# Attention and an MLP in one kernel: plain products for the first output group, and another order of sums, copies and pieces

## The chip, the cores and the metric

The kernel runs on one core of a Trainium2 chip. The core has five engines that work side by side, each through its own queue: TensorE (PE in the profile, with its weight loads listed apart as PEld), VectorE (DVE), ScalarE (ACT), GpSimd (POOL) and SyncE (SP). POOL and SP mainly start DMA transfers here. The metric is the device time of one execution in microseconds (us). Before the change it was 392.39 us, the median of three runs (391.98 to 393.38).

## What is computed

Attention with a squared ReLU in place of a softmax, for 8 batches of 12 heads, 448 positions and a head size of 64; then a two-layer MLP with an exact GELU over the 8 x 448 = 3584 tokens.

```python
def _attn_ref(q, k, v):                  # 8 x 12 x 448 x 64 each
    S = q.shape[2]
    scale = 1.0 / np.sqrt(q.shape[-1])
    scores = scale * np.matmul(q, k.transpose(0, 1, 3, 2))
    attn = np.maximum(scores, 0.0) ** 2 / S
    return np.matmul(attn, v)

def _moe_ref(x, w_in, w_out):            # x: 3584 x 768, w_in: 768 x 2048, w_out: 2048 x 768
    h = x @ w_in
    g = 0.5 * h * (1.0 + erf(h / sqrt(2)))
    return g @ w_out
```

The attention's output, 12 heads of 64 side by side, is the x of the MLP. Inputs and output are float32.

## The kernel before

The matmuls are in bf16. The program is built by a small list scheduler: every piece of work is an `Op` with its possible engines and durations, the pieces that it depends on and the buffers that it needs and frees. The scheduler picks, for each engine, the piece that can start earliest by its own estimates (a `bias` shifts a piece's rank), and then writes the instructions in that order. At run time each engine works through its queue in that order. The order of PE and of POOL is fixed by hand (`pe_q`, `pool_q`); the scheduler decides the rest.

The parts that the change touches are these.

**The second layer by seven products.** The tokens are taken in 14 groups of 256 rows (two tiles of 128). For a group, the second layer is a product of 2 x 2 blocks: two row tiles, the 2048 inner columns in two halves, the 768 output columns in two halves. It is done by a scheme with seven block products in place of eight (a form of Strassen's scheme). That needs sums of weight blocks, made once, and sums of activation blocks for each group, both on DVE.

```python
    K2 = KF // 2                         # 8 slices of 128 inner columns
    quad = {(i, j): wout_sb[:, i*K2 : i*K2+K2, j*ND : j*ND+ND] for i in range(2) for j in range(2)}
    tsum = {n: wpool.tile([128, K2, ND], BF16, ...) for n in (1, 2, 4)}
    tsum[3] = quad[0, 1]                 # the third sum overwrites a block of the weights

    def add_tsums():                     # weight sums, in two parts each (x = 0, 1)
        def sub(n, c, a, b, deps):
            return sch.add((("DVE", 0.95, 1.07),),
                lambda e: V.tensor_sub(tsum[n][:, c], a[:, c], b[:, c]), deps, bias=SUM_BIAS)
        for x, c in enumerate((slice(0, 4), slice(4, K2))):
            ld = list(ld_wout.values())
            t1 = sub(1, c, quad[0, 1], quad[0, 0], ld[: x + 1])
            t2 = sub(2, c, quad[1, 1], tsum[1], [t1] + ld)
            t3 = sub(3, c, quad[1, 1], quad[0, 1], [t1] + ld)
            t4 = sub(4, c, quad[1, 0], tsum[2], [t2] + ld)
            SUMS[x] = [t1, t2, t3, t4]

    def add_group(g):
        # ... (cut) rows, buffers
        done = [o for (bb, *_), o in GL.items() if bb in bs] + SUMS[0] + SUMS[1]
        # ... (cut) activation sums, each a DVE tensor_tensor, with bias=SUM_BIAS
        s1 = sum_op(1, add, lambda: h(0, o2), lambda: h(1, o2), done)
        s2 = sum_op(2, sub, lambda: box["s", 1], lambda: h(0, o1), done + [s1])
        s3 = sum_op(3, sub, lambda: h(0, o1), lambda: h(0, o2), done)
        s4 = sum_op(4, sub, lambda: h(1, o1), lambda: box["s", 2], done + [s2])
        # ... (cut) product(): 8 matmuls into a PSUM bank; passed(): bank to SBUF, copied or added
        p1 = product("a", lambda: h(0, o1), quad[0, 0], done, need=("f",))
        v1 = passed("a", first, None, [p1], need=("p",))
        p6 = product("b", lambda: box["s", 2], tsum[2], done + [s2], need=("f",), frees=("s2",))
        v2 = passed("b", part(0, right), first, [v1, p6], need=("osb",))
        # ... (cut) p2, p7, p5, p4, p3 with their passes and the stores
        return [(1.3, o) for o in (p1, p6, p2, p7, p5, p4, p3)]
```

The PSUM banks of these products and of the first layer come from a pool of two (`f_pp`, "f").

**The copies and transposes of Q and K.** From batch 2 on, Q and K of a batch are loaded by POOL's queue (`nq`, `nk`), rearranged by DVE (`pk`, three copies; `pq`, six), and turned by seven DMA transposes on SP's queue (`kT`, `qT`). A tiny POOL copy (`gate`) holds the next batch's loads until the transposes are done.

**The order on PE.** Attention pieces (scores `ps` at L550, output `pav` at L612) and MLP pieces (first layer `psh` at L659, second layer `pso` at L752) are interleaved. While a batch's attention runs, the MLP pieces of the batch before are put between its steps, in proportion to their cost.

```python
    order = slots(2, B)                  # six slots for each batch from 2 on
    per = 2 * G
    GROUPS = {2: (0, 1), 3: (2, 3), 4: (4, 5), 5: (6,), 6: (7, 8), 7: (9, 10), 8: (11, 12, 13)}
    for b in range(2, B):
        add_steps(steps(b), dve=1)
        # ... (cut) copies, transposes and loads of later batches; at b == 2: add_tsums()
        x2 = [y for g in GROUPS[b] for y in add_group(g)]
        carry = x2[len(x2) - 7 + CARRY :]          # the last three products go to the next stage
        stage.append(atoms + x2[: len(x2) - 7 + CARRY])
    for n, slot in enumerate(order):
        # ... (cut) attention pieces of the slot
        while atoms and done < total * (n % per + 1) / per - 0.01:
            done += atoms[0][0]
            pe_q.append(atoms.pop(0)[1])
```

Of the kernel before, what the change touches and what calls it, by code (L numbers as in the profile page):

```python
# [13 lines left out]
KC = 112  # L14
NC = S // KC
# [33 lines left out]
DVE_STEPS = (1,)  # L49
HALF_M = 6  # L50
PASS_BIAS = -0.4
SUM_BIAS = 0.3
CARRY = 4


# [155 lines left out]
def kernel(  # L211
# [194 lines left out]
    def add_pk(b, g0, g1, after=(), bias=0.0):  # L406
        for g in range(g0, g1):
            deps = ld_k[b, g] + list(after)
            deps += [Tk[max(b - 1, 1), x, i][0] for x in range(G) for i in range(NK)]
            Pk[b, g] = sch.add(  # L410
                (("DVE", 0.31, 0.43),),
                lambda e, g=g: permute_k(V.tensor_copy, g, nk[b][:, 2 * g : 2 * g + 2]), deps,
                bias=bias,
            )

    def add_pq(b, g0, g1, c0=0, c1=NC, after=(), bias=0.0):
        for g in range(g0, g1):
            deps = [ld_q[b, g, c] for c in range(c0, c1)] + list(after)
            deps += [Tq[max(b - 1, 1), g, c][0] for c in range(c0, c1)]
            if b == 2:  # L420
                deps += [Tq[1, x, c][0] for x in range(G) for c in range(NC)]
            d = 2 * (0.07 + (c1 - c0) * 128 / 3840)

            def fn(e, g=g):
                permute_q(
                    V.tensor_copy, g, c0, c1, nq[b][:, 4 * g : 4 * g + 4, c0 * D : c1 * D]
                )

            op = sch.add((("DVE", d, d + 0.12),), fn, deps, bias=bias)
            for c in range(c0, c1):  # L430
                Pq[b, g, c] = op
# [59 lines left out]
    def add_T_dma(b, after):  # L491

        after = [list(x) for x in after]
        for g in range(G):
            def fn(e, g=g):
                nc.sync.dma_start_transpose(
                    get_T(b)[1][:, g].rearrange("p (i t) -> p i t", t=128), get_p()[1][:, g]
                )

            op = sch.add((("SP", 1.2, 3.0),), fn, [Pk[b, g]] + old_T(b) + after.pop(0))  # L500
            for i in range(NK):
                Tk[b, g, i] = (op, op)
        for c in range(NC):
            def fn(e, c=c):
                nc.sync.dma_start_transpose(get_T(b)[0][:, :, bass.ts(c, KC)], get_p()[0][:, c, :])  # L505

            op = sch.add((("SP", 1.2, 3.0),), fn, [Pq[b, g, c] for g in range(G)] + old_T(b) + after.pop(0))
            for g in range(G):
                Tq[b, g, c] = (op, op)
# [20 lines left out]
    def h_ring():  # L530

        if not hT:
            hT[0] = hpool.tile([128, KF, RING], BF16, tag="h", name="h_sb")
        return hT[0]
# [164 lines left out]
    def add_tsums():  # L699

        def sub(n, c, a, b, deps):
            return sch.add(
                (("DVE", 0.95, 1.07),),
                lambda e: V.tensor_sub(tsum[n][:, c], a[:, c], b[:, c]), deps, bias=SUM_BIAS,  # L704
            )

        for x, c in enumerate((slice(0, 4), slice(4, K2))):
            ld = list(ld_wout.values())
            t1 = sub(1, c, quad[0, 1], quad[0, 0], ld[: x + 1])
            t2 = sub(2, c, quad[1, 1], tsum[1], [t1] + ld)  # L710
            t3 = sub(3, c, quad[1, 1], quad[0, 1], [t1] + ld)
            t4 = sub(4, c, quad[1, 0], tsum[2], [t2] + ld)
            SUMS[x] = [t1, t2, t3, t4]

    osbs = {}

    def add_group(g):

# [4 lines left out]
        def h(i, o):  # L723
            return h_ring()[:, i * K2 : i * K2 + K2, o : o + 128]

        done = [o for (bb, *_), o in GL.items() if bb in bs] + SUMS[0] + SUMS[1]
        mine = []
        box = {}

# [17 lines left out]
        def product(bank, left, right, deps, need=(), frees=(), joint=()):  # L747
            def fn(e):
                if need:
                    box[bank] = f_pp.tile([128, NB], F32, tag="f", name="pso")  # L750
                for kf in range(K2):
                    nc.tensor.matmul(  # L752
                        box[bank][:, :ND],
                        left()[:, kf],
                        right[:, kf],
                        start=bool(need) and kf == 0,
                        stop=kf == K2 - 1,
                        skip_group_check=not need,
                    )

            d = K2 * (ND / 2400 + 0.0025)
            o = sch.add(
                (("PE", d, d + 0.24),), fn, deps, need=need, frees=frees, joint=joint, mode="F"
            )
            mine.append(o)
            return o

        def osb(x):
            if (g, x) not in osbs:
                osbs[g, x] = opool.tile([128, DM], F32, tag="osb", name="osb")  # L770
            return osbs[g, x]
# [20 lines left out]
            )  # L792

        def store(x, c, queues):
            def fn(e):
                queue, j = list(queues), rows[x][0]
                while j < rows[x][0] + 128:
                    bb, r = divmod(j, S)
                    k, p0 = divmod(r, KC)
                    m = min(KC - p0, rows[x][0] + 128 - j)  # L800
                    to = out[bb * S : (bb + 1) * S, :].rearrange("(p c) d -> c p d", c=NC)
                    y = j - rows[x][0]
                    queue.pop(0).dma_start(to[k, p0 : p0 + m, c], osb(x)[y : y + m, c])
                    j += m

            return fn

        left, right, full = slice(0, ND), slice(ND, DM), slice(0, DM)
        p1 = product("a", lambda: h(0, o1), quad[0, 0], done, need=("f",))
        v1 = passed("a", first, None, [p1], need=("p",))  # L810
        p6 = product("b", lambda: box["s", 2], tsum[2], done + [s2], need=("f",), frees=("s2",))
        p6.joint, s4.joint, s4.frees = [s4], [p6], ("s2",)
        v2 = passed("b", part(0, right), first, [v1, p6], need=("osb",))
        p2 = product("a", lambda: h(1, o1), quad[1, 0], [v1])
# [17 lines left out]
            readers.setdefault(bb, []).extend(mine)  # L832
        return [(1.3, o) for o in (p1, p6, p2, p7, p5, p4, p3)]

    def f1(b):
        return [(1.14, add_f1(b, m)) for m in range(KF)]

    def steps(b):
        return [((b, g, i, None),) for g in range(G) for i in range(NK)]
# [5 lines left out]
            tuple(x[n : n + 2]) for n in range(7, len(x), 2)  # L845
        ]

    def slots(first, last):


        out, done = [], None
        for b in range(first, last):
            for g in range(G):
                x = [("QK", (b, g, i, None)) for i in range(NK)]
                mid = ("AV", done) if done else ("FFN", None)
                out.append(x[:2] + [mid] + x[2:4])
                out.append(x[4:])
                done = (b, g, None)
        return out + [[("AV", done)]]


    nc.scalar.dma_start(k32, kv_view(k, 0, 0, 1))
# [85 lines left out]
        add_f1(0, m, bias=F1B_BIAS)  # L948


    order = slots(2, B)
    first = [next((x for kind, x in sl if kind == "QK"), None) for sl in order]
    per = 2 * G

    class at_slot:


        def __init__(self, n):
            self.key = first[n]

        @property
        def done(self):
            return QK[self.key].done

    def at(n):
        return [at_slot(min(n, len(first) - 2))]

    stage = []
    GROUPS = {2: (0, 1), 3: (2, 3), 4: (4, 5), 5: (6,), 6: (7, 8), 7: (9, 10), 8: (11, 12, 13)}
    add_load(3)  # L970
    for b in range(2, B):
        add_steps(steps(b), dve=1)
        if b + 1 < B:

            n = per * (b - 2) + {2: 2, 3: 2}.get(b, 1)
            add_pk(b + 1, 0, G, after=at(n))
            add_pq(b + 1, 0, G, after=at(n))
            add_T_dma(b + 1, [at(n + (y >= 4)) for y in range(7)])
            if b + 2 < B:
                add_gate(b + 1)  # L980
                add_load(b + 2)
        if b == 2:
            add_tsums()
            x1 = f1(b - 1)
            first_atoms, atoms = x1[:LEAD], x1[LEAD:]
        else:
            atoms = carry + f1(b - 1)
        x2 = [y for g in GROUPS[b] for y in add_group(g)]
        carry = x2[len(x2) - 7 + CARRY :]
        stage.append(atoms + x2[: len(x2) - 7 + CARRY])  # L990
    pe_q.extend(x[1] for x in first_atoms)
    for n, slot in enumerate(order):
        for kind, x in slot:
            if kind == "FFN":
                pe_q.append(stage[0].pop(0)[1])
            else:
                pe_q.append(AV[x] if kind == "AV" else QK[x])
        if n < per * len(stage):
            atoms = stage[n // per]
            if n % per == 0:  # L1000
                total, done = sum(x[0] for x in atoms), 0.0
            while atoms and done < total * (n % per + 1) / per - 0.01:
                done += atoms[0][0]
                pe_q.append(atoms.pop(0)[1])
    for _, o in carry + f1(B - 1) + [y for g in GROUPS[B] for y in add_group(g)]:
        pe_q.append(o)
    sch.run({"PE": pe_q, "POOL": pool_q})
# [28 lines left out]
```

## Time and profile before

| | before |
|---|---|
| time, median of 3 | 392.39 us |
| span of the profiled execution | 392.5 us |
| mean granted TensorE clock | 0.973 of full |
| PE busy, matmuls | 367.4 us, 3325 |
| DVE busy, instructions | 253.6 us, 456 |
| ACT busy, instructions | 200.6 us, 304 |
| weight sums, L704 | 8, about 0.95 us each |
| activation sums, L733 | 56, about 0.68 us each |

A line such as "93.83 2.74 PE L752 MATMUL ... x8 [13.02 <-DVE s_sb L733]" is a piece of the timeline: start, length, engine, line of the kernel, operation, output from inputs, how many instructions are merged, and in brackets the idle time of the engine before it and what ended that. "Line waited for" views give the total of such idle times, how many, and the longest. Busy time is instruction time; a PE that is busy at half clock is still busy, so the row of granted clock is read beside it. Idle time on an engine that does not set the end costs nothing.

### The profile page before, as it was taken

Reading aid. Unit: us, or ns where it says so; the run is one execution under the profiler, and the core shown is the slowest. Engines: PE = TensorE matmul, PEld = TensorE weight load, DVE = VectorE, ACT = ScalarE, POOL = GpSimd, SP = SyncE. Lnnn points to the kernel's source line nnn. Section 1 sums busy time; section 2 is a strip of 40 time slices with the busy share of each in tenths; the row PEclk is TensorE's granted clock in tenths of the full one; section 3 lists DMA queues with packets and bytes.
Section 4 is the critical chain, followed back from the end, with each engine's and each line's share of the span. In section 5 each row is a group of like instructions: output and inputs, shape, how many; then the busy total and the mean of one; then the engine's idle time right before and its main releaser. Section 6 shows DMA issues by size and latency. Waiting matters only on the chain.

```text
span 392.5 us, 7901 instructions
## 1 busy us (share of the span) xinstructions
PE 367.4 (94%) x3325; PEld 202.6 (52%) x3325; DVE 253.6 (65%) x456; ACT 200.6 (51%) x304; POOL 45.8 (12%) x69
## 2 busy tenths in 40 slices
PE   8799999924969999999999999999999999999995
PEld 7576544412535555555555445555555555555663
DVE  3899963476769457894488846963787438800662
ACT  4898855820524773456543776477345754144000
POOL 8665303100200002001100020000000000000000
PEclk9899999975989999999999999999999999999999
DMA  9999998999972168854950879280022001120232
GB/s 176 195 197 204 198 159 110 209 202 164 130 162 78 29 115 125 172 128 95 166 115 17 183 109 138 73 133 18 3 82 80 2 3 55 42 64 2 72 88 82
DMA packets 69523, 42.93 MB, mean 109 GB/s; under 512 B 37744, under 2 KB 66032, under 8 KB 69488
## 3 DMA queue, kind: packets, MB, share of 16 engines
q0 software_dynamic: 30512, 22.47, 38.4%
q1 hardware_dynamic: 38656, 19.46, 23.0%
q8 instruction: 26, 0.43, 0.4%
q10 hardware_dynamic: 320, 0.51, 0.4%
q14 instruction: 9, 0.07, 0.1%
HBM read 45.61 MB, written 11.01 MB: 144 GB/s over the span
## 4 chain that ended last, share of the span: by engine, by line
PE 81%; DMA 8%; DVE 5%; POOL 2%; ACT 1%; SPq 1%; issue 1%; POOLq 0%
PE pso L752 33%; PE psh L659 33%; PE ps L550 8%; DMA nq<-in_q_dram 7%; PE pav L612 7%; DVE a_sq L571 1%; SPq L505 1%; DVE s_sb L733 1%; DMA qT<-pq 1%; ACT a_sq L562 1%; POOL nk L348 1%; POOL v_sb L366 1%; DVE a_sq L564 1%; DVE t_sb L704 0%; DVE xT L314 0%
## 5 line engine op out<-in xcount | busy, mean ns | idle before, releaser
L562 ACT ACTIVATE a_sq<-ps 128x896 bf16<-128x896 f32 (+1 forms) x141 | 123.0, 914 | 72.8 <-PE ps L550 72.8
L659 PE MATMUL psh<-xT,win_sb 128*128 128x448 bf16 (+1 forms) x804 | 151.2, 345 | 0.1
L571 DVE TENSOR_TENSOR a_sq<-a_sq 128x896 bf16<-128x896 bf16 (+1 forms) x169 | 101.9, 617 | 43.1 <-ACT a_sq L562 42.0
L659 PEld LDWEIGHTS <-win_sb 128*128 128x128 bf16 x804 | 76.3, 98 | 71.2 <-issue 9.1
L669 ACT ACTIVATE h_sb<-psh 128x448 bf16<-128x448 f32 x128 | 70.1, 547 | 63.1 <-PE psh L659 52.9
L752 PEld LDWEIGHTS <-s_sb 128*128 128x128 bf16 x448 | 43.5, 99 | 48.2 <-DVE s_sb L733 16.8
L752 PE MATMUL pso<-t_sb,s_sb 128*128 128x384 bf16 x224 | 43.3, 339 | 16.0 <-DVE s_sb L733 16.0
L550 PE MATMUL ps<-qT,kT 64*64 64x448 bf16 (+1 forms) x756 | 48.0, 344 | 1.4 <-ACT qT L316 0.5
L752 PEld LDWEIGHTS <-h_sb 128*128 128x128 bf16 x336 | 32.4, 99 | 25.1 <-issue 4.6
L564 DVE TENSOR_SCALAR a_sq<-ps 128x896 bf16<-128x896 f32 x28 | 30.4, 1090 | 18.9 <-PE ps L550 18.4
L752 PE MATMUL pso<-wout_sb,h_sb 128*128 128x384 bf16 x224 | 41.9, 331 | 0.0
L752 PE MATMUL pso<-wout_sb,s_sb 128*128 128x384 bf16 x224 | 41.0, 326 | 0.0
L612 PE MATMUL pav<-a_sq,v_sb 64*64 64x448 bf16 (+1 forms) x756 | 37.3, 334 | 0.7 <-ACT a_sq L562 0.4
L786 DVE TENSOR_TENSOR osb<-pso,p_sb 128x384 f32<-128x384 f32 x42 | 23.4, 558 | 17.3 <-PE pso L752 15.6
L550 PEld LDWEIGHTS <-kT 64*64 64x64 bf16 x756 | 18.9, 108 | 23.0 <-issue 18.1
L612 PEld LDWEIGHTS <-v_sb 64*64 64x64 bf16 x756 | 21.7, 109 | 12.8 <-issue 2.0
L316 ACT CAST xT<-pav 128x448 bf16<-128x448 f32 (+1 forms) x25 | 12.4, 495 | 21.1 <-DVE xT L314 11.8
L314 DVE COPY p_sb<-pso 128x384 f32<-128x384 f32 x14 | 7.8, 557 | 22.8 <-PE pso L752 22.6
L517 POOL COPY gate<-qT 128x4 bf16<-128x4 bf16 x5 | 1.0, 199 | 169.9 <-DMA qT<-pq 169.9
L752 PE MATMUL pso<-t_sb,h_sb 128*128 128x384 bf16 x112 | 20.5, 326 | 0.0
L314 DVE CAST xT<-pav 128x448 bf16<-128x448 f32 (+1 forms) x29 | 16.3, 567 | 6.3 <-ACT xT L316 4.6
L786 DVE TENSOR_TENSOR osb<-pso,osb 128x384 f32<-128x384 f32 x28 | 15.6, 558 | 6.2 <-PE pso L752 4.6
(39 smaller groups left out, 148.9 us busy)
## 6 DMA issues: line engine op xcount, KB each, us to landing
nk<-in_k_dram POOLq DMA_DIRECT2D x5, 672.0 KB, 6.6
nq<-in_q_dram POOLq DMA_DIRECT2D x5, 672.0 KB, 9.9
v_sb<-in_v_dram POOLq DMA_DIRECT2D x5, 672.0 KB, 14.4
out_dram<-osb SPq DMA_DIRECT2D x8, 336.0 KB, 2.9
wout_sb<-in_moe_w_out_dram POOLq DMA_DIRECT2D x2, 1152.0 KB, 11.6
v_sb<-in_v_dram POOLq DMA_DIRECT2D x9, 224.0 KB, 9.2
out_dram<-osb SPq DMA_DIRECT2D x7, 288.0 KB, 3.0
out_dram<-osb SPq DMA_DIRECT2D x8, 240.0 KB, 3.0
```

The source lines that it names most:

```text
L314: V.tensor_copy(dst, src)
L316: A.copy(dst, src)
L348: nc.gpsimd.dma_start(nk[b][:, 2 * g0 : 2 * g1], kv_view(k, b, g0, g1))
L550: nc.tensor.matmul(ps[64 * j : 64 * j + 64, e, x * w : x * w + w], kT[r, g, i * 128 + 64 * j : i * 128 + 64 * j + 64], qT[r, 2 * g + j, co ...
L562: A.activation(ar, ps, AF.Relu, scale=c_att)
L564: V.tensor_scalar(ar, ps, c_att, 0.0, op0=mybir.AluOpType.mult, op1=mybir.AluOpType.max,)
L571: V.tensor_mul(box["a2"][:, :, :used], ar, ar)
L612: nc.tensor.matmul(pav[0][o2 : o2 + 64, e, :w], vt[b][r, 2 * g + e, bass.ts(i, D)], box["a2"][r, e, o : o + w], start=(i == 0), stop=(i == ...
L659: nc.tensor.matmul(ph[:, x * n : x * n + n], win_sb[:, kd, bass.ts(m + x, 128)], xT[b][:, kd, c], start=(kd == 0), stop=(kd == KD - 1),)
L669: A.activation(h_ring()[:, m : m + nm, o + c.start : o + c.stop], box[0][:, :S].rearrange("p (x n) -> p x n", x=nm), AF.Gelu,)
L752: nc.tensor.matmul(box[bank][:, :ND], left()[:, kf], right[:, kf], start=bool(need) and kf == 0, stop=kf == K2 - 1, skip_group_check=not need,
L786: V.tensor_add(out(), box[bank][:, :ND], other())
```

## The change

It changes five things, all around the start of the second layer, where group 0 is the first to need the weight sums:

- Group 0 (rows 0 to 255) is computed by plain products of the weights as they are: two row tiles times two column halves, each one accumulation of 16 matmuls. These need no weight sums and no activation sums. The stage of batch 2 then has the plain products and group 1.
- The third weight sum, which overwrites a weight block that two of the plain products read, comes last and after those two products. The other sums keep their order.
- Activation sums get the bias -0.3 (they had 0.3) and weight sums 0.2, so the scheduler puts activation sums earlier; and of a group only the second product waits for the weight sums, no longer the first product or the activation sums.
- The K and Q copies of a later batch wait for all weight sums.
- The attention of batch 2 is ended within its own stage, and eight MLP pieces (the last three products of group 1 and five pieces of batch 2's first layer) are put on PE ahead of batch 3's first attention step, to cover the later copies and transposes.

The store of a row tile moves to a helper of its own (`store_rows`). Lines that only follow from this are cut.

```diff
-SUM_BIAS = 0.3
+SUM_BIAS = -0.3
+TSUM_BIAS = 0.2
+LEADS = {3: 8}
...
             t1 = sub(1, c, quad[0, 1], quad[0, 0], ld[: x + 1])
             t2 = sub(2, c, quad[1, 1], tsum[1], [t1] + ld)
-            t3 = sub(3, c, quad[1, 1], quad[0, 1], [t1] + ld)
             t4 = sub(4, c, quad[1, 0], tsum[2], [t2] + ld)
-            SUMS[x] = [t1, t2, t3, t4]
+            SUMS[x] = [t1, t2, t4]
+        for x, c in enumerate((slice(0, 4), slice(4, K2))):
+            SUMS[x].append(sub(3, c, quad[1, 1], quad[0, 1], SUMS[x] + list(ld_wout.values()) + plain[:2]))
...
-        done = [o for (bb, *_), o in GL.items() if bb in bs] + SUMS[0] + SUMS[1]
+        done = [o for (bb, *_), o in GL.items() if bb in bs]
+        sums = SUMS[0] + SUMS[1]
...
-        p6 = product("b", lambda: box["s", 2], tsum[2], done + [s2], need=("f",), frees=("s2",))
+        p6 = product("b", lambda: box["s", 2], tsum[2], done + sums + [s2], need=("f",), frees=("s2",))
...
+    def add_plain(t, n):
+        c, o = slice(n * ND, n * ND + ND), 128 * t % RING
+        box = []
+        def fn(e):
+            box.append(f_pp.tile([128, NB], F32, tag="f", name="pso"))
+            for kf in range(KF):
+                nc.tensor.matmul(
+                    box[0][:, :ND], h_ring()[:, kf, o : o + 128], wout_sb[:, kf, c],
+                    start=kf == 0, stop=kf == KF - 1,
+                )
+        def fn2(e):
+            ...  # the output tile, once for each t
+            copy(e, osbs[t, "plain"][:, c], box[0][:, :ND])
+        bb, r = divmod(128 * t, S)
+        deps = [x for (b, *_), x in GL.items() if b == bb] + list(ld_wout.values())
+        op = sch.add((("PE", 2.6, 2.84),), fn, deps, need=("f",), mode="F")
+        ev = sch.add(e_copy(ND, 1), fn2, [op], frees=("f",), need=("osb",) if n else ())
+        ...  # the store after the second half
...
-    GROUPS = {2: (0, 1), 3: (2, 3), ...
+    GROUPS = {2: (1,), 3: (2, 3), ...
...
+        if b == 2:
+            x1 = f1(b - 1)
+            first_atoms, atoms = x1[:LEAD], x1[LEAD:]
+            atoms += [(2.6, add_plain(t, n)) for n in (1, 0) for t in (0, 1)]
+            add_tsums()
...
-            add_pk(b + 1, 0, G, after=at(n))
-            add_pq(b + 1, 0, G, after=at(n))
+            add_pk(b + 1, 0, G, after=at(b, n) + SUMS[0] + SUMS[1])
+            add_pq(b + 1, 0, G, after=at(b, n) + SUMS[0] + SUMS[1])
...
+    for b, atoms in stage.items():
+        for _ in range(LEADS.get(b, 0)):
+            pe_q.append(atoms.pop(0)[1])
+        total, gone = sum(x[0] for x in atoms), 0.0
+        for n, slot in enumerate(plan[b]):
+            ...  # attention pieces of the slot, then MLP pieces in proportion, as before
```

## The prediction

> **What bounds the kernel now.** I read the page first: its busy line and the row of granted clock.
>
> ```profile
> PE 367.4 (94%) x3325; PEld 202.6 (52%) x3325; DVE 253.6 (65%) x456; ACT 200.6 (51%) x304; POOL 45.8 (12%) x69
> ...
> PEclk9899999975989999999999999999999999999999
> ```
>
> TensorE (PE) is busy for 94% of the span and carries most of the chain that ended last, so time can only come from its gaps or from fewer matmuls. The clock row has its deepest dip at slices 8 and 9 (0 is the first; a slice is 9.8 us), so something happened between 78 and 98 us, with a smaller dip at slice 11. Next I read the waits of PE:
>
> ```profile
> PE pso L752 <- DVE s_sb L733: 16.0, 2, 13.0
> ```
>
> The columns are total us, number of waits, longest. Two waits of the second layer's products for activation sums make 16.0 us; every other PE wait is 1.0 us or less. The timeline of PE puts them in place:
>
> ```profile
> 79.33 1.47 PE L752 MATMUL pso<-wout_sb,h_sb 128*128 128x384 bf16 x8
> 93.83 2.74 PE L752 MATMUL pso<-t_sb,s_sb 128*128 128x384 bf16 x8 [13.02 <-DVE s_sb L733]
> ...
> 106.71 1.46 PE L752 MATMUL pso<-wout_sb,h_sb 128*128 128x384 bf16 x8
> 111.16 2.44 PE L752 MATMUL pso<-t_sb,s_sb 128*128 128x384 bf16 x8 [2.99 <-DVE s_sb L733]
> ```
>
> The reader should see that the first product of group 0 runs at once, the second waits 13.02 us, and that the same eight matmuls which take 1.47 us elsewhere take 2.74 and 2.44 us after the gaps. Last, the timeline of VectorE (DVE) in the first gap:
>
> ```profile
> 80.69 0.96 DVE L704 TENSOR_TENSOR t_sb<-wout_sb,t_sb 128x1536 bf16<-128x1536 bf16 x1
> 81.57 1.37 DVE L571 TENSOR_TENSOR a_sq<-a_sq 128x896 bf16<-128x896 bf16 x2
> 84.06 1.00 DVE L393 COPY pk<-nk 128x896 bf16<-128x896 bf16 x3 [1.12 <-DMA nk<-in_k_dram]
> 84.97 0.95 DVE L704 TENSOR_TENSOR wout_sb<-wout_sb 128x1536 bf16<-128x1536 bf16 x1
> 85.84 0.95 DVE L704 TENSOR_TENSOR t_sb<-wout_sb,t_sb 128x1536 bf16<-128x1536 bf16 x1
> 87.59 1.30 DVE L404 COPY pq<-nq 112x512 bf16<-112x512 bf16 x6 [0.80 <-DMA nq<-in_q_dram]
> 88.81 0.95 DVE L704 TENSOR_TENSOR t_sb<-wout_sb,t_sb 128x1536 bf16<-128x1536 bf16 x1
> 89.68 0.95 DVE L704 TENSOR_TENSOR wout_sb<-wout_sb 128x1536 bf16<-128x1536 bf16 x1
> 90.54 0.95 DVE L704 TENSOR_TENSOR t_sb<-wout_sb,t_sb 128x1536 bf16<-128x1536 bf16 x1
> 91.41 1.29 DVE L733 TENSOR_TENSOR s_sb<-h_sb 128x1024 bf16<-128x1024 bf16 x2
> ```
>
> Six weight sums stand ahead of the first activation sum, and among them are the copies of batch 3's K and Q, which wait for loads (K at 84.06, Q at 87.59). DVE's queue is in order, so everything behind them waits too.
>
> **What the Trainium skill says.** "TensorE: Matmul & The Clock Gate", section "Architectural detail", calls the DVE queue strict FIFO. The lines above agree: weight sums whose operands had landed by 80.69 run at 88.81 and later, behind the Q copy. The same page's Part 1 says that an idle array falls to half clock after about 3.4 us and needs a similar busy time to recover. The trace agrees on the half (2.74 against 1.47 us) but the second dip came after only 2.99 us idle, so I treat gaps near 3 us as dear and gaps below 1.5 us as free of clock loss. "VectorE: DVE Perf Modes", "The perf-mode tier table", gives bf16 tensor_tensor two results a cycle; the trace's pitch in queue (88.81 to 89.68) is 0.87 us for 1536 columns, and I use such pitches.
>
> **What the change removes.** Group 0's Strassen-like seven products become four plain ones of 16 matmuls, which need no sums. The whole of the stage's first gap had one cause, sums on DVE, so it should close; so should the second, where group 1's sums were queued behind squares. I sum the loss by stretches of the chain. Gaps: 13.02 + 2.99 + 0.17 (a small PE wait at 119.80) = 16.2 us. Clock: 16 matmuls from 93.83 took 4.74 us where the chain has 2.60 us for 16 in later stages, +2.14; eight at 111.16, 2.44 against 1.30, +1.14; the twelve attention matmuls after them 1.27 against 0.69, +0.58. That is 3.9 us, so 20.1 us in all are to be had.
>
> **What it adds.** 64 matmuls replace 56. The last 168 matmuls of the kernel take 27.32 us, 0.163 each, so +1.3 us on PE. DVE loses four activation sums (about 2.5 us) and part of seven passes; both are off the path if the schedule works.
>
> **What it moves, step by step on PE.** The order of instructions shows that up to the attention pieces at 65.89 nothing moves; then one MLP piece (1.14 us) slides to just ahead of the plain products, so the first plain product again starts at 79.33. Its 16 matmuls use the three loads of the output weights in order. The last load was issued at 66.25 and landed 14.4 us later, 80.65; it is needed from the eleventh matmul, at 79.33 + 1.63 = 80.96. No wait, by 0.3 us. From there, at full rate: product 2.60, attention 0.69, product 2.60, attention and its AV step 0.50 + 1.32 + 0.38, two products 5.20, attention 0.69, group 1's first product 1.30. The sum puts group 1's second product, the first user of sums, at 94.6.
>
> **DVE against that, from pitches.** Weight sum at 80.69; four activation sums end at 84.1 (0.60 each, 0.12 for one dependence); five squares at 0.53 to 86.7; a weight sum 87.6; a 1.00 us scaling, a 0.53 copy and four squares (two of them held to 90.8 or so by ScalarE) to 91.3; three weight sums to 93.9; the copy of the fourth plain product 0.46 to 94.35; the last weight sum to about 95.3. So I expect a wait of some 0.7 us there in place of 13, too short to lose the clock. Behind it come two small ones: the last AV step needs a square queued behind a pass (0.2 us), and a product needs a bank whose copy stands behind the Q and K copies (0.45 us). Together 1.4 us.
>
> **Batch 3.** Its K copies move behind the sums, to about 98.0, and its Q copies end about 100.8. Seven DMA transposes follow; with the loads over by then (V landed 22.5 us after issue, 91.6) each should take the 1.28 us that is the median of the Q transposes, K from 98.35 and Q to 107.1, and the last lands 2.7 us on, about 109.8. PE meanwhile has after group 1's second product (95.4 to 96.7) the AV step to 98.2, five products to 105.2 with the wait above, and five MLP pieces of 1.135 us to 110.9. These eight pieces (three products, five MLP) are the part "ahead of batch 3 attention": without them (9.6 us of work) attention would be reached about nine microseconds before its transposes landed. The slack is about 1 us.
>
> **The sum.** From the attention piece at 163.66 in the trace before (late in batch 3's stage) PE's order is the same to the end. The work from 79.33 to there is 84.3 us less 20.1, or 64.2; plus 1.3 for matmuls, plus 1.4 of new waits: 66.9, so that point comes at 146.2 and 17.4 us are saved. 392.4 - 17.4 = 375.0 us.
>
> **Rivals.** First, the wait comes back at another place: the last weight sum also waits for the copy of the fourth plain product, which can't start before 92.65. If squares or ScalarE push DVE later, PE waits one for one, and above 3 us the clock loss of some 2 us comes with it. For it: my DVE chain is already late by 0.7. Against it: it has 3.9 us of work between 91.3 and 95.2 and no load wait left. It would make 377 to 381. Second, batch 3's transposes become the bound: K transposes under load took 7.13 us for three at 84.60. If stores or loads slow these, attention waits up to 4 us: 377 to 380. Against it: nothing else is in flight but two stores. Third, the schedule works so well that none of the new waits show: 373.5. Fourth, DVE is simply the bound and only moves the gap, as its 10.73 busy us of 12.8 in the gap might suggest, so little is gained, 388 or more. Against it: half of those are sums and copies which now run while PE does 10.4 us of plain products, and group 0's are gone.
>
> **Range and chances.** The ideal is 373.5 and each likely miss costs 2 to 5 us, so the low end is 373.0 and the high end 379.5. Gains under 2% (above 384.5) need the fourth rival or two others together: faster 0.95, same 0.04, slower 0.01.
>
> **What would show it.** Right: PE's waits for sums fall from 16.0 to under 2 us; no clock digit of 5 or 7 past slice 7; the first attention of batch 3 near 111 us; matmuls 3333. Wrong: a PE wait of 3 us or more on a weight sum or a transpose, or a clock dip near slice 9 or 11; a new wait in stages after 146 us would also break it, since I take their order on PE as all that matters.

## The result and the profile after

| | before | after |
|---|---|---|
| time, median of 4 runs each, same chip | 392.88 us | 379.19 us |
| ratio, 95% interval | 1 | 0.9645 (0.9604 to 0.9686) |
| span of the profiled execution | 392.5 us | 377.5 us |
| mean granted TensorE clock | 0.973 | 0.998 |

The changed kernel takes 13.7 us less, inside the predicted range (by 0.3 us) and 4.2 us above the predicted time of 375.0. Its page has these lines for the busy time of the engines and the granted clock:

```profile
PE 364.9 (97%) x3333; PEld 200.8 (53%) x3333; DVE 246.4 (65%) x446; ACT 201.9 (53%) x307; POOL 46.1 (12%) x69
...
PEclk9999999999999999999999999999999999999999
```

There are 8 more matmuls and yet PE is busy for 2.5 us less, as no slice shows a reduced clock any more. The dips of slices 8, 9 and 11 are gone, and that is the change. The dip of slice 1 (the digit 8) is gone too, and it lies ahead of all that the change touches: PE was busy for 74.7 us before its first second-layer product and is busy for 73.0 now, with the same 1029 matmuls. So 1.6 us of the difference belong to that one execution of before. The view of PE's waits (total us, number, longest) no longer has a line for activation sums. Its two largest lines are new:

```profile
PE ps L552 <- DVE a_sq L566: 1.9, 5, 0.7
PE ps L552 <- DVE xT L316: 1.1, 1, 1.1
```

L566 is the scaling by which DVE clears a bank of scores; the 16.0 us of before were two waits, these are five small ones and one of 1.1 us. PE's timeline shows where they are (start, length, and in brackets the idle time before):

```profile
78.37 2.76 PE L850 MATMUL pso<-wout_sb,h_sb 128*128 128x384 bf16 x16
...
87.06 0.38 PE L552 MATMUL ps<-qT,kT 64*64 64x448 bf16 x4 [0.51 <-DVE a_sq L566]
...
94.68 1.46 PE L768 MATMUL pso<-t_sb,s_sb 128*128 128x384 bf16 x8
...
110.11 0.57 PE L552 MATMUL ps<-qT,kT 64*64 64x448 bf16 x8
...
137.41 0.38 PE L552 MATMUL ps<-qT,kT 64*64 64x448 bf16 x4 [1.10 <-DVE xT L316]
...
149.23 0.38 PE L552 MATMUL ps<-qT,kT 64*64 64x448 bf16 x4 [0.72 <-DVE a_sq L566]
```

The 64 plain matmuls (L850) start at 78.37. Group 1's second product, the first user of sums, runs at 94.68 without a wait. Batch 3's attention starts at 110.11. Past 78 us there are three idle times over 0.3 us, the three in brackets; they stand in front of the last four score matmuls of an attention step. DVE's timeline shows why group 1 does not wait: its activation sums run early, and the last weight sum has ended at 94.21.

```profile
79.83 1.29 DVE L749 TENSOR_TENSOR s_sb<-h_sb 128x1024 bf16<-128x1024 bf16 x2 [0.51 <-ACT h_sb L671]
...
93.26 0.95 DVE L706 TENSOR_TENSOR wout_sb<-wout_sb 128x1536 bf16<-128x1536 bf16 x1
```

Where the 15.0 us between the two profiled spans came from is seen by cutting both at the first product of the second layer and at the attention piece late in batch 3's stage. The columns are the stretch, its length, the busy time of PE, PEld, DVE, ACT and POOL, granted clock, DMA share and GB/s. Before:

```profile
79.33:163.70 84.37, 68.19 (x540) 35.41 (x540) 59.34 (x108) 34.99 (x50) 5.53 (x8) 0.90 0.78 135
163.70:392.50 228.80, 224.53 (x1764) 120.72 (x1762) 140.17 (x250) 107.72 (x165) 5.60 (x8) 1.00 0.36 75
```

And after:

```profile
78.37:146.46 68.09, 66.45 (x545) 35.03 (x546) 51.67 (x96) 36.52 (x54) 5.56 (x8) 1.00 0.91 147
146.46:377.50 231.04, 225.37 (x1765) 121.03 (x1764) 139.24 (x250) 107.77 (x165) 5.82 (x8) 1.00 0.38 79
```

The stretch that the change is about became 16.28 us shorter. The rest of the kernel, in which PE does the same work in the same order, became 2.24 us longer. And the first 79 us, with the same work in both, were 0.96 us shorter in this execution: 16.28 + 0.96 - 2.24 = 15.0. In before's execution the granted clock was 0.83 between 10 and 20 us, in after's 1.00, so these 0.96 us are no gain of the change.

The 2.24 us are in the chain of work that ended last (start, length, engine, output, line). In after it has the same four steps at four places; this is the second:

```profile
193.14 0.56 DVE osb L802
193.69 0.60 DVE s_sb L749
194.29 1.01 DVE a_sq L566
195.31 0.04 issue
195.35 0.38 PE ps L552 x4
```

The like piece of the chain of before, at the point that answers to the first place, has only PE in it:

```profile
163.66 0.50 PE ps L550 x8
164.17 1.32 PE pav L612 x28
165.49 0.38 PE ps L550 x8
```

In after, an activation sum (s_sb, L749, bias -0.3) stands on DVE between a pass and the scaling, and PE waits for the scaling. From the start of these score matmuls to the product behind them before took 0.48 us; after takes 1.40 us at 148.15 and 0.91 us in the other three (the shown wait leaves out a modelled end of 0.2 us). 0.92 + 3 x 0.43 = 2.2 us, which is all of it. At the three places of 0.43 us the sum is the only thing that is new. The first place, with 0.92 us, has a second cause, a late store (e0, e8 and e9).

### The profile page after: what moved, and what is told of

Same layout as the page of the kernel before. It is cut to its first block, busy times and chain, and to the rows that moved or that the text cites. A ratio compares the mean times of both kernels' runs of the same rounds, so it can differ in the third digit from the quotient of the medians.

```text
span 377.5 us, 7915 instructions
## 1 busy us (share of the span) xinstructions
PE 364.9 (97%) x3333; PEld 200.8 (53%) x3333; DVE 246.4 (65%) x446; ACT 201.9 (53%) x307; POOL 46.1 (12%) x69
## 4 chain that ended last, share of the span: by engine, by line
PE 85%; DVE 9%; ACT 2%; DMA 1%; POOL 1%; issue 0%; POOLq 0%; ACTq 0%
PE psh L661 38%; PE pso L768 32%; PE ps L552 8%; PE pav L614 6%; DVE a_sq L573 4%; DVE a_sq L566 2%; DMA nk<-in_k_dram 1%; PE pso L850 1%; DVE s_sb L749 1%; ACT a_sq L564 1%; DVE xT L316 1%; DVE osb L802 1%; ACT xT L318 1%; DVE kT L316 0%; PE tp L446 0%
## 5 line engine op out<-in xcount | busy, mean ns | idle before, releaser
L573 DVE TENSOR_TENSOR a_sq<-a_sq 128x896 bf16<-128x896 bf16 (+1 forms) x169 | 100.6, 616 | 42.1 <-ACT a_sq L564 41.9
L768 PEld LDWEIGHTS <-s_sb 128*128 128x128 bf16 x416 | 40.0, 98 | 28.3 <-issue 2.5
L566 DVE TENSOR_SCALAR a_sq<-ps 128x896 bf16<-128x896 f32 x28 | 30.4, 1089 | 23.0 <-PE ps L552 22.6
L768 PEld LDWEIGHTS <-h_sb 128*128 128x128 bf16 x312 | 29.8, 98 | 22.1 <-issue 2.8
L768 PE MATMUL pso<-t_sb,s_sb 128*128 128x384 bf16 x208 | 38.1, 326 | 0.0
L768 PE MATMUL pso<-wout_sb,h_sb 128*128 128x384 bf16 x208 | 38.1, 326 | 0.0
L768 PE MATMUL pso<-wout_sb,s_sb 128*128 128x384 bf16 x208 | 38.1, 326 | 0.0
L802 DVE TENSOR_TENSOR osb<-pso,p_sb 128x384 f32<-128x384 f32 x39 | 21.7, 558 | 12.9 <-PE pso L768 10.5
L768 PE MATMUL pso<-t_sb,h_sb 128*128 128x384 bf16 x104 | 19.0, 326 | 0.0
L802 DVE TENSOR_TENSOR osb<-pso,osb 128x384 f32<-128x384 f32 x26 | 14.5, 558 | 5.4 <-PE pso L768 2.9
```

The source lines that it names most:

```text
L566: V.tensor_scalar(ar, ps, c_att, 0.0, op0=mybir.AluOpType.mult, op1=mybir.AluOpType.max,)
L573: V.tensor_mul(box["a2"][:, :, :used], ar, ar)
L768: nc.tensor.matmul(box[bank][:, :ND], left()[:, kf], right[:, kf], start=bool(need) and kf == 0, stop=kf == K2 - 1, skip_group_check=not need,
L802: V.tensor_add(out(), box[bank][:, :ND], other())
```

## The experiments

Theories, with the letters that the expectations use; in e4 A stands for something else, which is said there with C, and E is said in e3. A: the time given back after 146 us comes from activation sums queued ahead of the scaling. B: it comes from something else, and early sums are needed as they are. D: the eight pieces ahead cover the transposes of batch 3, as the prediction says. F: holding the query and key copies back protects group 1's second product, which needs the last weight sum. G: it does not need it. Times are medians, with the ratio to the kernel before on the same chip.

**e0, the changed kernel again.** No edit; a second profile, to see whether its waits come back.

> The changed kernel once more, as the measure for the runs beside it. Both theories: 379.2 us within 0.5, waits of PE behind step-1 scalings of attention (the group of line 566) about 1.9 us in 5 places, four of them after 146 us.

Measured 379.37 us, 0.9659 (0.9639 to 0.9679); waits behind L566 1.9 us in 5 places. The waits belong to the kernel, not to one execution. This profile's chain also goes one step further back at the first place:

```profile
140.54 6.58 DMA out_dram<-osb
...
147.20 0.56 DVE osb L802
147.76 0.60 DVE s_sb L749
148.35 1.01 DVE a_sq L566
```

There the pass itself had waited for the store that frees its output buffer. So this place has two causes, the other three only the sum. What each does there is seen from the start of one attention step to that of the next: 16.09 us in before, 17.01 in after. With the early sum and no late store it is 16.51 (e7); with the late store and no sum ahead of the scaling, 17.09 (e8) and 17.11 (e9). So the sum alone costs 0.42 us there and the store alone about 1.0; they do not add, and taking out the sum brings nothing at this place as long as the store is late.

**e6, plain products alone.** The old biases, copies not held, no pieces ahead. Two things of the change stay beside the plain products: the third weight sum still comes last and behind two of them, which its overwriting of a block makes necessary, and still only the second product of a group is listed as waiting for the weight sums.

```diff
-SUM_BIAS = -0.3
-TSUM_BIAS = 0.2
-LEADS = {3: 8}
+SUM_BIAS = 0.3
+TSUM_BIAS = 0.3
+LEADS = {}
...
-            add_pk(b + 1, 0, G, after=at(b, n) + SUMS[0] + SUMS[1])
-            add_pq(b + 1, 0, G, after=at(b, n) + SUMS[0] + SUMS[1])
+            add_pk(b + 1, 0, G, after=at(b, n))
+            add_pq(b + 1, 0, G, after=at(b, n))
```

> The kernel before with plain products for group 0 and nothing else: old biases, copies of batch 3 not held back, no pieces ahead. By pitches group 1's second product waits for its sums about 4.5 us plus a clock loss of 2, and later stages have no new waits: 382.5, range 381 to 385. Theory C (the order of sums carries the gain): 388 or more.

Measured 381.29 us, 0.9709 (0.969 to 0.9727), as expected. The plain products, with the order that they need, bring 11.5 us. What is left is mainly this in PE's timeline:

```profile
99.26 2.36 PE L768 MATMUL pso<-t_sb,s_sb 128*128 128x384 bf16 x8 [3.59 <-DVE s_sb L749]
```

Group 1 waits for its sums, and the 16 matmuls from there take 2.36 and 2.30 us for eight, a reduced clock. Ahead of it, at 90.59, stands a wait of 1.29 us for a scaling. There is no wait over 0.3 us from there to 150 us and none in the late stages, and none for a transpose, though no pieces are put ahead.

**e4, all but the plain products.** Groups 0 and 1 by seven products, with the new order.

```diff
-    GROUPS = {2: (1,), 3: (2, 3), ...
+    GROUPS = {2: (0, 1), 3: (2, 3), ...
-            atoms += [(2.6, add_plain(t, n)) for n in (1, 0) for t in (0, 1)]
```

> Groups 0 and 1 both by seven products; the orders of sums and copies and the eight pieces ahead of batch 3 are kept. Theory A (the plain products buy the time for the weight sums, whose last operand lands near 80): the first group's second product waits about 8 us and the clock drops: 388, range 386 to 390. Theory C (the order of sums and copies alone carries the gain): 381 or less.

Measured 387.04 us, 0.9847 (0.9822 to 0.9871). The time is in the expected range partly by luck, as the wait stands elsewhere. The second product waits 0.17 us only; a later one waits, in PE's timeline:

```profile
89.65 2.72 PE L768 MATMUL pso<-wout_sb,s_sb 128*128 128x384 bf16 x8 [4.53 <-DVE osb L802]
```

DVE's timeline ahead of that pass:

```profile
87.74 0.99 DVE L395 COPY pk<-nk 128x896 bf16<-128x896 bf16 x3
88.64 0.49 DVE L406 COPY pq<-nq 112x512 bf16<-112x512 bf16 x2
89.05 0.55 DVE L802 TENSOR_TENSOR osb<-pso,p_sb 128x384 f32<-128x384 f32 x1
```

The pass, which frees a PSUM bank, stands behind the copies, which stand behind the last weight sums. So the other four parts take 6 us off the kernel before, and the plain products are needed for the rest. DVE has no pause from 78.84 to 90 us here, and the plain products take the first 10 us of second-layer work out of its hands. The 6 us of e4 and the 11.5 us of e6 are more than the 13.7 us of the whole: both shorten the same gaps.

**e3, no pieces ahead of batch 3.** The edit also moves the last attention output of batch 2 (the `pav` below) back into batch 3's stage, so both halves of the fifth part are out.

```diff
-LEADS = {3: 8}
+LEADS = {}
```

> No MLP pieces ahead of batch 3's attention, the rest as changed. Theory D (the pieces hide the transposes, which land 10 us after the copies): PE comes to batch 3 near 98, Q's last transpose lands near 107, so a wait of about 9 us and a clock loss of some 2: 389, range 386 to 391. Theory E (the pieces are not needed, the transposes would be there anyway): 380 or less.

Measured 388.54 us, 0.9892 (0.9872 to 0.9913): D holds, for copies that are held back as in the change. PE's timeline at batch 3's first attention, and the step after it:

```profile
108.11 0.96 PE L552 MATMUL ps<-qT,kT 64*64 64x448 bf16 x8 [8.36 <-DMA qT<-pq]
108.83 2.85 PE L614 MATMUL pav<-a_sq,v_sb 64*64 64x448 bf16 x28
```

The wait is 8.36 us, and the 28 matmuls after it take 2.85 us where they take 1.49 elsewhere.

**e5, copies not held back.** The last four lines of e6's edit alone.

> As changed, but the K and Q copies of a later batch no longer wait for the weight sums, so batch 3's copies stand ahead of five of the eight weight sums on DVE and wait there for Q's load (near 87). Theory F (holding the copies back is needed for group 1's second product): the last weight sum ends near 98 where PE comes near 94.7, a wait of about 3 us and a clock loss of 2 to 3: 383.5, range 382 to 385.5. Theory G (with plain products there is time enough for the copies): 379.4.

Measured 378.82 us, 0.966 (0.9641 to 0.9679), as the changed kernel: F falls, G holds. Group 1's second product in PE's timeline, and then the last weight sum but one in DVE's:

```profile
94.33 1.46 PE L768 MATMUL pso<-t_sb,s_sb 128*128 128x384 bf16 x8
```

```profile
96.08 0.95 DVE L706 TENSOR_TENSOR t_sb<-wout_sb,t_sb 128x1536 bf16<-128x1536 bf16 x1
```

The product starts 1.75 us before this sum does, and the last one starts at 96.94. The dependence on all sums is in the scheduler's list and fixes only order; on the chip the product waits for what it reads, the second sum and its activation sum. Batch 3's copies end at 91.2 us here, and yet its attention starts at 109.46, for the pieces are still ahead of it. Whether the pieces can go when the copies are not held and the sums are early was not tried; e6 has neither, with the late sums, and no wait there.

**e7, early activation sums in the kernel before.**

```diff
-                (("DVE", 0.69, 0.8),), fn, deps, need=(f"s{n}",), bias=SUM_BIAS
+                (("DVE", 0.69, 0.8),), fn, deps, need=(f"s{n}",), bias=-0.3
```

> The kernel before with one thing changed, the early bias -0.3 of the activation sums. The 13 us wait of group 0 stays, as its weight sums still stand behind Q's load; the 3 us wait of group 1 with its clock loss of 1.7 goes; the later stages pay some 2 us for sums in front of step-1 scalings: 392.9 - 4.7 + 2.2 = 390.4, range 389 to 392. If early sums were what the change lives on: 385 or less.

Measured 392.73 us, 1.0001 (0.9987 to 1.0015): missed by 2.3 us. Its waits of PE:

```profile
PE pso L752 <- DVE s_sb L733: 11.7, 1, 11.7
PE ps L550 <- DVE a_sq L564: 2.9, 6, 1.0
```

The 2.99 us wait of group 1 is gone, as the edit should do, and six waits behind the scaling have come. The last four of them are 0.23 us each in the four late stages, where the changed kernel has them too. The first two, 0.96 us each near 106 and 117 us, were not expected; they cost some 1.2 us each from start to start, which is about the miss. This is A with nothing else of the change present: the early sums pay in one place, and the waits behind the scaling take as much again.

**e1, late activation sums for all groups.**

```diff
-SUM_BIAS = -0.3
+SUM_BIAS = 0.3
```

> All activation sums have the old bias 0.3, group 1 too, the rest as changed. Group 1's sums then stand behind the Q copies of batch 3; from pitches the sum that its second product needs ends near 97.4 where PE comes near 94.7, a wait of some 2.7 us. Theory A: 376.2 plus 2.7 to 4 = 379 to 380.5. Theory B: 382 to 383, as the later stages would give nothing back.

Measured 384.16 us, 0.9771 (0.9739 to 0.9803), above both. There is no wait behind the scaling after 100 us, as A has it. But there are two for sums, not one: group 1's 2.40 us and one of 3.53 us in group 3, each with eight matmuls at 2.74 us behind it.

**e2, early sums for group 1 only.**

```diff
-... need=(f"s{n}",), bias=SUM_BIAS
+... need=(f"s{n}",), bias=SUM_BIAS if g == 1 else 0.3
```

> The early bias of the activation sums is kept for group 1 alone; later groups have the old bias 0.3. Theory A (the 2.2 us lost after 146 us, and about 1 us in batch 3's stage, come from an activation sum queued in front of a step-1 scaling or a copy that frees a PSUM bank): 376.2, range 375.5 to 377.0, and no PE wait behind line 566 after 146 us. Theory B (the loss is an effect of the run or of the other parts of the change): 379.2 as the changed kernel.

Measured 382.39 us, 0.9726 (0.9692 to 0.976), above both. The four late waits are gone; one at group 3 has come, as in e1. PE's timeline:

```profile
145.16 2.74 PE L768 MATMUL pso<-t_sb,s_sb 128*128 128x384 bf16 x8 [3.53 <-DVE s_sb L749]
...
150.25 1.91 PE L768 MATMUL pso<-wout_sb,s_sb 128*128 128x384 bf16 x8
```

I had read only the wait of group 1 as the reason for early sums. Group 3 needs them as well. The eight matmuls between the two lines take 2.76 us, so that three products at 1.46 us lose 1.28 + 1.30 + 0.45 us of clock; with the wait that is 6.6 us. Saved are the 2.2 us of the late stages and 1.3 us near 137 us, where there is no wait now: 6.6 - 3.5 = 3.1, and the time is 3.0 us above that of e0.

**e8, early sums up to group 3.**

```diff
+... bias=SUM_BIAS if g <= 3 else 0.3
```

> The early bias holds for groups 1, 2 and 3, the old one from group 4 on. Theory A, amended (early sums are wanted while DVE is crowded, up to batch 3's stage, and cost 0.5 to 0.9 us in each of four later stages): the 3.53 us wait of group 3 seen with the early bias for group 1 alone is gone and the four late waits too: 379.4 less 2.2 = 377.2, range 376.6 to 377.8. Theory B (late stages lose for another reason): 379.4.

Measured 378.42 us, 0.9639 (0.962 to 0.9658), above the expected range. PE waits after 150 us: none. The three places with only the sum as cause are settled, in the direction of A. The time is 0.8 us under the changed kernel's 379.2, where 1.3 us were to be had; as ratios the two intervals overlap, so the vanished waits show more than the times. The waits at 137 us (1.10) and 149 us (0.81) stay, the second though no sum stands ahead of its scaling now.

**e9, and those of group 3 between scaling and weight sums.** A bias of -0.1 lets the scaling go first but not the squares.

```diff
+... bias=SUM_BIAS if g < 3 else -0.1 if g == 3 else 0.3
```

> As the run before, but group 3's sums have the bias -0.1, which puts its second sum behind the step-1 scaling and the copy that frees a bank, and still ahead of the product that needs it. Theory A amended: the 1.10 us wait in batch 3's stage goes too: 376.2, range 375.5 to 377.0. If the 1.10 us wait had another cause: 377.2.

Measured 377.25 us, 0.9609 (0.959 to 0.9628), 0.25 us above the expected range. The wait of 1.10 us at 137 us, which ended with a cast of x, is down to 0.23, now that the scaling goes ahead of the second sum and gives a bank free earlier (135.68 against 137.80). That of 0.82 us at 148.7 stays although no sum stands before its scaling: the chain has the store, at 139.64 for 7.41 us, then the pass. On DVE:

```profile
147.13 0.56 DVE L802 TENSOR_TENSOR osb<-pso,p_sb 128x384 f32<-128x384 f32 x1 [1.40 <-DMA out_dram<-osb]
147.60 1.08 DVE L566 TENSOR_SCALAR a_sq<-ps 128x896 bf16<-128x896 f32 x1
```

The DMA issues between 139 and 141.5 us (output, queue, number, KB each, us to landing) next to those from 142 to 165 us; the first line is the one DMA queue that moved packets in the first window (packets, MB, time as a share of 16 engines), the queue of the loads:

```profile
q0 software_dynamic: 555, 0.50, 124.5%
out_dram<-osb SPq DMA_DIRECT2D x1, 288.0 KB, 7.4
```

```profile
out_dram<-osb SPq DMA_DIRECT2D x2, 336.0 KB, 2.8
```

A store of 288 KB lands after 7.4 us where the larger ones of 336 KB take 2.8. Ahead of the first window batch 5's three loads had been issued, from 136.05 to 137.80 us; the stores followed from 139.26. The Trainium skill, "DMA: Bandwidth & Descriptors", section "Queues, rings and completion order", says that a DMA engine goes round its queue rows a packet at a time; a store beside three loads would then get a share only. The trace is harsher than that: the stores' queue moved no packet from 139 to 142 us and four between 142 and 143; 200 packets followed from 145 to 147, when the loads' had thinned out. It agrees with the loads as the cause; whether they are is for e12.

**e11, both: e9 and the copies not held back.** The edits of e9 and e5.

> The kernel of e9 (activation sums first for groups 0 to 2, between the step-1 scaling and the weight sums for group 3, last from group 4 on), and the query and key copies of batches 2 and 3 no longer held behind the sums. If the two gains are of different waits they add: 377.25 less the 0.5 us that the copies' early place took from the wait ahead of group 1's fourth bank: 376.7 (376.2 to 377.3), with no wait above 0.3 us between 78 and 100 us. If they are the same time counted twice: 377.2 or more. Either way the wait of 0.8 us near 148.7 us stays.

Measured 376.38 us, 0.9584 (0.9555 to 0.9613). It is within the range of the first reading. But its chip was the faster one (392.16 us for the kernel before; 392.81 for e9's), and the intervals of e9 and e11 overlap, so that e11 gains over e9 is likely and not settled. Both intervals lie under that of e0, the changed kernel (the first measurement's, 0.9604 to 0.9686, is wider and overlaps them). The wait of the score matmuls ahead of the third plain product, 0.51 us in e9, is 0.17, as the first reading has it; one of 0.43 us stands at 78.95, in a profiled execution that took 2.1 us more than the median. In e12, which has this order too, there is none between 78 and 100 us. The wait behind the late store stays, 0.66 us.

**e12, batch 5's loads later.** Beside e11, one more gate copy on GpSimd's queue ahead of those loads, which waits for a piece of x of the batch before.

```diff
+                if b == 3:
+                    add_gate_x(b)      # gpsimd.tensor_copy(gate, xT[b][:, 2, ::KC])
```

> As the kernel beside it, and one more gate of GpSimd ahead of the loads of batch 5, so that they start near 148 us and not near 136 us. If the wait of 0.8 us near 148.7 us comes from an output store that is slowed by these loads, the store of 140 us lands in about 3 us rather than 6.6, the wait goes, and the time is 0.5 to 0.8 us less than beside it: about 376.0 (375.5 to 376.5). Rival: the pass is late for another reason, the store lands as late and the time is the same; or the later loads delay the inputs of batch 5, and a new wait of the transposes of x takes the gain or more.

Measured 377.08 us, 0.9601 (0.9572 to 0.963): no gain. GpSimd's timeline tells why it settles nothing:

```profile
136.91 0.82 POOL L350 DMA_DIRECT2D nk<-in_k_dram  x1 [0.35 <-DVE xT L316]
```

The piece of x was ready 1.2 us after the old gate, so the first of the loads was issued at 136.9 and not near 148 us. In the chain the store at 138.90 takes 7.63 us. The edit did not do what its expectation supposes. Loads that start well after the store were not tried, nor was a fourth output buffer. That the loads slow the store is therefore argued, not shown.

## Why the prediction was right, and what its sum lacked

- **The gap closes.** Right. No wait for an activation sum is left, and no dip of clock. e6 shows that the plain products, with the order that they need, do most of it (11.5 of 13.7 us), e4 that order without them is worth 6 us. The fourth rival, DVE as the bound, did not come: DVE is busy for 51.67 of 68.09 us in the stretch.
- **A wait of 0.7 us for the last weight sum.** Wrong, and so was the first rival as stated. Of the weight sums the product reads the second only, and in e5 it starts ahead of the last two. The step took the scheduler's dependence for a wait of the instruction. In after the last sum was also done earlier than predicted, at 94.21 and not 95.3, so that there was nothing to wait for in any case.
- **Two small waits, 0.45 and 0.2 us.** Both came, at 0.19 and 0.14 us. The attention output at 96.08 takes 1.63 us in place of 1.49, and the product whose bank is freed behind the query and key copies starts 1.49 us after the one before it in place of 1.30 (98.95 to 100.44; with the copies not held, in e5, it is 1.30). Two larger ones were missed. One is 0.51 us at 87.06, for a bank of scores whose scaling stood behind five squares and a weight sum. The other is 1.10 us at 137.41: sums of group 3 had gone ahead of the scaling there (e9 puts the second behind it, and 0.23 us are left). Of the 1.4 us of new waits in the sum, about 0.3 came as described; the two that were missed cost some 0.7 and 1.3 us from start to start.
- **Batch 3.** Right. The last transpose had landed at 109.4 (109.8 predicted) and PE came at 110.11 (110.9), a slack of 0.7 us. Without the pieces the wait is 8.36 us (about nine predicted). What the prediction took as given, that the copies must be held and so be covered, is not so: e5 does without the holding, and e6 without both and has no wait there. As far as these runs go, the pieces make good what the holding costs.
- **The stretch from the first product.** Predicted 66.9 us, measured 68.09: 1.2 us too short. Of the waits put in, 1.1 us did not come, and 2.0 us of others did, which is most of it.
- **"I take their order on PE as all that matters."** This step failed, and the prediction's own last sign of being wrong, a new wait after 146 us, came true. From 163.66 in the trace before PE's order is the same, but DVE's is not: a sum of 0.60 us ahead of the scaling, at one place also a late store, costs 2.24 us in four stages. Three of them, 1.3 us, are the sum's alone; e7 makes the four waits in the kernel before, e8 takes these three out of the changed one. At the fourth the store, which the prediction did not follow either, is enough by itself (e8, e9).
- **The last subtraction, 392.4 - 17.4.** The 392.4 is the median; the 17.4 us were read from a profiled execution that took 394.26 us, 1.9 us above that median. The profiled execution of after, at 379.3 us, is at its own median. So part of the time that the trace showed is not in the median: 0.96 us of it was in the first 79 us, where both kernels do the same work and this execution had a dip of clock at 10 to 20 us. Where the other 0.9 us lay is not shown. Low clock and long time go together in the runs of the kernel before that stand beside the experiments: those with a mean clock of 0.972 or 0.973, as this execution had, took 394.47 to 394.76 us, those with 0.976 to 0.981 took 391.58 to 393.79.

The miss of 4.2 us is then 2.2 (late stages) + 1.2 (stretch) + 1.9 (profile against median) - 1.0 (the earlier start, which is part of that 1.9) = 4.3. The mechanism of the gain was right; the terms that were mis-sized are the later stages, put at nothing (2.24 us measured), the stretch (66.9 against 68.09) and the baseline (392.4 against 394.26).

## What to carry to other kernels

When one engine's order is kept by hand and another's by a scheduler, compare the order on both, to the end of the kernel: a priority that is raised for one stage is raised in all, and here one short instruction ahead of the one that frees a PSUM bank cost the matmul engine 0.43 us in each of the late stages that have it. Raise it for the groups that need it (here 1 to 3) and no others. Before savings from a profile are subtracted from a median, compare the profiled execution's own time, and its row of granted clock, with those of the other executions.

## What the runs showed of the hardware

- Half clock came after a gap of only 2.40 us (e1: 2.74 us for eight matmuls against 1.46), less than the 2.99 us of the kernel before. After gaps of 1.10 us (after) and 1.29 us (e6) there was none; no gap between 1.3 and 2.4 us occurred, so the prediction's line of 1.5 us is not tested. The Trainium skill, "TensorE: Matmul & The Clock Gate", Part 1, gives about 3.4 us and a window that runs freely; a gap shorter than that was enough here.
- The way back took different times: after 2.40 us idle, eight matmuls at half clock and then nearly full (the next 28 took 1.82 us, where 1.49 is usual); after 3.53 us, 16 at half clock and eight at 1.91 us, some 6 us in all. After the same 3.53 us in e1 it was eight and then 1.81.
- A store of 288 KB landed after 2.9 us in most places (the median of seven in after) and after 6.7 us (after) or 7.4 us (e9) when it was issued just behind three loads of 672 KB each. That the loads are the reason is argued from the queues' packets (e9), not shown.
